# First-read touch, K of the first tile by chunks, a tile copied by two engines, and two more product slots, in an attention-plus-gated-MLP kernel

## The chip, the cores and the metric

The kernel runs on one core of one Trainium2 chip. The time is device microseconds of an execution. Spans inside a profile count from the first instruction of the profiled execution to the last, and are some 2 us shorter than the execution's time (269.8 us beside 271.54 for the profiled run of the kernel before).

PE is the matrix engine, DVE the vector engine, ACT the scalar engine, POOL the general one. SP issues most transfers. PSUM is the memory whose banks PE writes its results to, SBUF the working memory of all engines.

## The reference

```python
xn = layernorm(x)                      # x: [1, 2048, 640] bf16
q, k, v = split(xn @ wqkv)             # 32 heads of 20; wqkv: [640, 1920]
# each position s sees 8 keys: s, s-2, ..., s-14
attn = softmax(q . k[s - 2*w] * 20**-0.5)
A = (sum over w of attn * v[s - 2*w]) @ wo
B = ((xn @ w_gate) * (xn @ w_up)) @ w_down    # 640 -> 1536 -> 640
out = x + A + B
```

## The kernel before

The program has its own scheduler: while it is built, it estimates when each task could start, and so fixes the order of instructions on every engine. The program hands each engine its instructions in that order, with waits on semaphores between them. The order therefore matters as much as the work.

The start. Tiles of 128 rows of `x` and the columns of `wqkv` for Q, K and V are loaded on one queue, in this order. The small "touch" reads 64 bytes of every fifth row of `wqkv` in advance, on the queue of ACT, with no other use:

```python
    x_load(0)
    tch = A_wqkv.rearrange("(p r) n -> p r n", r=NCH)[:, 0, 0:32]
    stores.append(dma(TCH[:], tch, w=[TCH[:]], name="touch", eng="act"))
    x_load(1)
    wqkv_load(0, 0, 3)       # Q columns, chunks 0 to 2 of 5 (480 KB)
    wqkv_load(0, 3, NCH)     # Q columns, chunks 3 and 4 (320 KB)
    x_load(2)
    wqkv_load(1)             # K columns, all five chunks (800 KB)
    x_load(3)
```

A tile is normalised on DVE and ACT (`stats` in two halves, then `aggr`, `sqrt`, `recip`, `apply`), transposed by PE into PSUM and copied to SBUF (`XNT`) by DVE. Then PE makes Q and K from it.

The middle. For each block j of 512 positions, DVE multiplies Q with shifted views of K into "product slots" of 4 KB per partition, and PE sums them over the head by matmuls with a 0/1 matrix (`logits`, the line of `G`). For the last block, j = 3, DVE writes 16 half-size products in fp32 (`PRF`), which are summed pairwise: four sums by transfers with an adding destination, the others by POOL. Each product needs a free slot, and a slot comes free when a sum has read it:

```python
                for c in (c0, c0 + 1):
                    yield lambda: len(hold[c]) > 0 and len(usable(j)) > 0
                    k = slot(j)
                    ...
                    yield Task("dve", go, r=[q, rk], w=[o[:]], prio=20 + j)
    def sum32(j, r, q0, p, a, b):
        x, y = PRD32[a][:], PRD32[b][:]
        if (r, q0) in BY_DMA[p]:
            yield Task("pool", lambda: op("pool", lambda e: e.dma_start(x, y, accum_op=ALU.add), ...))
        else:
            yield calm
            yield Task("pool", lambda: op("pool", lambda e: e.tensor_tensor(x, x, y, ALU.add), ...))
        free.append(b)
```

At the same time PE computes the gate and up matmuls of the MLP (`WG`, `WU`), and DVE multiplies them (`HT`), which frees their PSUM banks.

Of the kernel before, what the change touches and what calls it, by code (L numbers as in the profile page):

```python
# [4 lines left out]
BF16 = mybir.dt.bfloat16  # L5
# [44 lines left out]
class Sched:  # L50
# [77 lines left out]
    def op(self, eng, fn, r=(), w=(), dma=False, name="", occ=None, lat=None, lock=False, nbytes=0, mode=0, group=None, extra=0.0, acc=0.0):  # L128
        X = _Op()
        X.eng, X.fn, X.name, X.dma, X.group = eng, fn, name, dma, group  # L130
        X.needs_tick, X.event, X.pre_know, X.idx = False, None, None, len(self.ops)
        X.nth = self.n_eng[eng]
        self.n_eng[eng] += 1
        rk = [k for a in r for k in self.keys(a)]
        wk = [k for a in w for k in self.keys(a)]
        deps = self.deps_of(eng, rk, wk)
        if occ is None and not dma:
            occ = 0.1
        inorder = eng in ("pe", "act", "dve")
        start = max([self.t[eng]] + [d.end for d in deps.values()])  # L140
        if lock:
            start = max(start, self.t_lock)
        if eng == "pe" and mode != self.pe_mode:
            start += 0.1
            self.pe_mode = mode
        if dma:
            self.t[eng] = start + (0.48 if occ is None else occ)
            if acc:
                self.t_acc = max(self.t_acc, start + 2.8) + acc
                X.end = self.t_acc  # L150
            else:
                self.t_data = max(self.t_data, start + 1.2) + nbytes / 280e3
                X.end = self.t_data + 0.8 + extra
        else:
            self.t[eng] = start + occ
            X.end = start + (occ if lat is None else lat)
        if lock:
            self.t_lock = start + occ
        last = {}
        keep = []  # L160
        for d in deps.values():
            if d.dma or d.eng == "pool":
                keep.append(d)
            else:
                b = last.get(d.eng)
                if b is None or b.idx < d.idx:
                    last[d.eng] = d
        X.deps = keep + list(last.values())
        for d in X.deps:
            if not d.dma:  # L170
                d.needs_tick = True
        for k in rk:
            st = self.state.get(k)
            if st is None:
                self.state[k] = [None, [X]]
            elif inorder and st[1] and st[1][-1].eng == eng and not st[1][-1].dma:
                st[1][-1] = X
            else:
                st[1].append(X)
        for k in wk:  # L180
            self.state[k] = [X, []]
        if dma:
            if group is None or group not in self.groups:
                sem = self.nc.alloc_semaphore(f"dma{self.n_dma}")
                self.n_dma += 1
                if group is not None:
                    self.groups[group] = [sem, []]
            if group is None:
                X.event = (sem, 16)
            else:  # L190
                g = self.groups[group]
                g[1].append(X)
                X.event = (g[0], 16)
        self.ops.append(X)
        return X
# [151 lines left out]
def build_kernel(nc, A_x, A_wqkv, A_wo, B_x, B_w_gate, B_w_up, B_w_down, out):  # L347
# [58 lines left out]
    ATX = [ATX0, sb("ATX1", [128, 2, 2, JB])]  # L406
    PRD += [sb("PRD10", [128, 4, JB], at=place[0] - 4096), sb("PRD11", [128, 4, JB], at=place[0])]
    NPR = len(PRD)
    PRD32 = [K.sbuf(f"PRF{i}", [128, 2, JB], FP32, K.base[p.name]) for i, p in enumerate(PRD)]
    QUAD = {3: (1, 0)}  # L410
    BY_DMA = (((0, 0), (0, 2)), ((1, 0), (1, 2)))
# [9 lines left out]
    MV = sb("MV", [128, NT, 2], FP32)  # L421
    SD = sb("SD", [128, NT, 4], FP32)
    DUM = sb("DUM", [128, 16], FP32)
    TCH = sb("TCH", [128, 32])
    ZERO = sb("ZERO", [128, JB])
    EPSC = sb("EPSC", [128, 16], FP32)
    IDENT = sb("IDENT", [128, 128])
# [15 lines left out]
    def mark(*k):  # L443
        done.add(k)
# [84 lines left out]
    def front(t):  # L529
# [5 lines left out]
        def stats(i):  # L535
            o, a = st[:, 6 * i:6 * i + 6], x[:, i * DHALF:(i + 1) * DHALF]
            op("dve", lambda e: e.bn_stats(o, a), r=[a], w=[("st", t, i)], name=f"bn{t}_{i}", occ=0.49)  # L537
# [25 lines left out]
        if t == 1:  # L563
            yield have("sd", 0)
        for i in range(2):
            yield Task("dve", lambda: stats(i), r=[x], prio=-1 if t == 1 and i == 0 else p)
        yield Task("dve", aggr, r=[("st", t, 1)], prio=p)
        yield Task("act", sqrt, r=[("mv", t)], prio=p - 1)
# [5 lines left out]
        if t < N_PE_T:  # L574
            hold = []

            def trans(b):
                tpv = PS[:, b, :].bitcast(BF16)[:, 0:NCH * 128].rearrange("p (c f) -> p c f", c=NCH)
                for c in range(NCH):
                    i, q = xs[:, c * 128:(c + 1) * 128], tpv[:, c, :]  # L580
                    op("pe", (lambda q, i: lambda e: e.transpose(q, i, IDENT[:]))(q, i), r=[i, IDENT[:]], w=[q],  # L581
                       name=f"tr{t}_{c}", occ=0.057, lat=0.2)
                hold.append((b, tpv))
                if t == 0:
                    warm(3)

            def copy():
                b, tpv = hold[0]
                if t < N_DVE_C:
                    X = op("dve", lambda e: e.tensor_copy(o, tpv), r=[tpv], w=[o], name=f"xntcp{t}", occ=0.49)  # L590
                else:
                    X = op("act", lambda e: e.activation(o, tpv, ACT.Copy), r=[tpv], w=[o], name=f"xntcp{t}", occ=0.75)
                K.free_bank(b, X)

            yield Task("pe", trans, r=[xs], prio=p, banks=1)
            yield Task("dve" if t < N_DVE_C else "act", copy, r=[PS[:, hold[0][0], :]], prio=p)
        else:
            def dmat():
                op("sp", lambda e: e.dma_start_transpose(o, xs), r=[xs], w=[o], dma=True, name=f"dtr{t}", nbytes=200e3, occ=1.25, extra=1.3)

            yield Task("sp", dmat, r=[xs], prio=1)
# [9 lines left out]
            return WQKV[:, WPOS[2], c, m * 128:(m + 1) * 128]  # L611
        return WQKV[:, WPOS[which], c, m:D:NCH]

    def mms(parts, b, name):
        order = [(p, c) for p in parts for c in range(NCH)]
        if name == "p0_0":
            order.sort(key=lambda t: t[1])
        for k, ((o, which, m, s0, n), c) in enumerate(order):
            if True:
                first = c == 0  # L620
                l, x = wcols(which, c, m), XNT[:, c, s0:s0 + n]
                op("pe", (lambda o, l, x, c, first: lambda e: e.matmul(o, l, x, start=first, stop=(c == NCH - 1)))(o, l, x, c, first),  # L622
                   r=[l, x], w=[o], name=f"{name}_{m}_{c}", occ=n / 2400 + 0.0024, lat=0.3)
# [16 lines left out]
    def proj_group(items, s0, n, prio, keys):  # L640
        hold = []

        def spread(*bs):
            b = bs[0]
            assert list(bs) == list(range(b, b + 4))
            mms([(PS[:, x, 0:n], 0, k, s0, n) for k, x in enumerate(bs)], b, "p0_0")
            hold.append((b, [(qk_dst(0, 0, 4, s0, n), PS[:, b:b + 4, 0:n], 4 * n)]))

        def go(b):
            parts, outs, col = [], [], 0  # L650
# [15 lines left out]
                    for u in range(n // TS):  # L666
                        bump("qk", which, (s0 + u * TS) // JB, m0 + k)

        w0 = wcols(items[0][0], NCH - 1, 0)
        wide = prio == FIRST  # L670
        yield Task("pe", spread if wide else go, r=[w0, XNT[:, NCH - 1, s0 + n - TS:s0 + n]], prio=prio, banks=4 if wide else 1, contig=wide)
        yield Task("act", ev, r=[o for _, o, _ in hold[0][1]], prio=5)

    def proj_qk():
        for pair in (0, 2):
            for which in (0, 1):
                for t in (pair, pair + 1):
                    yield have("xnt", t)
                    K.spawn(proj_group([(which, 0, 4)], t * TS, TS, FIRST if t + which == 0 else 10, None))
            for which in (0, 1):  # L680
                K.spawn(proj_group([(which, 4, 1)], pair * TS, 2 * TS, 10.2, None))
        for t in (4, 6):
# [152 lines left out]
    def sum32(j, r, q0, p, a, b):  # L835
        x, y = PRD32[a][:], PRD32[b][:]
        name = f"qsum{j}_{r}_{q0}_{p}"
        if (r, q0) in BY_DMA[p]:
            yield Task("pool", lambda: op("pool", lambda e: e.dma_start(x, y, accum_op=ALU.add), r=[x, y], w=[x], dma=True,
                                          name=name, occ=0.88, acc=3.3), r=[x, y], w=[x], prio=4)  # L840
        else:
            yield calm
            yield Task("pool", lambda: op("pool", lambda e: e.tensor_tensor(x, x, y, ALU.add), r=[x, y] + tokens(), w=[x],  # L843
# [24 lines left out]
    def logits(j, slots):  # L868
# [32 lines left out]
                        m = LOG[0][0:32, 0, 4 * r + s, 0:DIL * w]  # L901
                        op("pool", (lambda m: lambda e: e.memset(m, NEG))(m), w=[m], name=f"mask{w}", occ=0.2)  # L902

        yield Task("pe", go, r=[e[1][:] for e in slots], prio=9.5, banks=2, slack=0.5)
        bump("lg")
        for r in (1, 0):
            yield Task("act", lambda: ev(r), r=[PS[:, hold[1 - r], :]], w=[dst(r)], prio=2)
# [2 lines left out]
    def softmax(x):  # L910
# [47 lines left out]
        yield Task("dve", recip, r=[s3], prio=10)  # L958
        yield Task("dve", attn, r=[R], w=[L[:]], prio=10, lock=True)
        mark("sm", x)  # L960
        yield Task("sp", move, r=[L[:]], prio=4)

    NU = NJ * NCH
# [281 lines left out]
    N_PE_T = 5  # L1245
    N_DVE_A = 6
    N_DVE_C = 5
    FIRST = 9
    GU_KEEP = 3
    HP_MAX = 2  # L1250
# [5 lines left out]
    FIN_PRIO = 8  # L1256

    x_load(0)
    tch = A_wqkv.rearrange("(p r) n -> p r n", r=NCH)[:, 0, 0:32]
    stores.append(dma(TCH[:], tch, w=[TCH[:]], name="touch", eng="act"))  # L1260
    x_load(1)
    wqkv_load(0, 0, 3)
    wqkv_load(0, 3, NCH)
    x_load(2)
    wqkv_load(1)
    x_load(3)
    K.t["act"] = 2.1
    warm(18)
# [69 lines left out]
```

## Time and profile before

The kernel before took 271.62 us (median of 3 runs, 271.34 to 272.56).

| | before |
|---|---|
| PE, DVE, ACT, POOL busy | 97%, 83%, 39%, 48% |
| chain of waits, by engine | PE 86%, DMA 5%, POOL 3% |
| PE time lost in the first 10 us | 2.1 us in three gaps |
| PE time lost from 100 to 116 us | 1.6 us in three gaps |

First, two lines of the page: busy time with its share of the span and instruction count, for each engine; then the chain of work that ended last, by engine.

```profile
PE 262.3 (97%) x1765; PEld 152.2 (56%) x1783; DVE 223.3 (83%) x283; ACT 104.6 (39%) x186; POOL 129.2 (48%) x80
...
PE 86%; DMA 5%; POOL 3%; DVE 2%; issue 2%; ACT 0%; SPq 0%; POOLq 0%; ACTq 0%
```

PE is the limit nearly all the time. But a busy share says little here: the Trainium skill, "Trainium Kernel Development and Optimization", section "Performance Expectations", warns that matmul busy time is a bad metric for how close a kernel is to the roofline, because matmuls are pipelined. So I also took, from the trace, each matmul's start minus the start before it, less the usual spacing. The Trainium skill, "TensorE: Matmul & The Clock Gate", section "Wait — 56ns, not 53.3ns?", gives that spacing, once the array is at full clock, as N / 2.4 GHz plus about 2.5 ns, 55.6 and 215.7 ns for 128 and 512 columns. This trace agrees (granted clock 1.00): the commonest spacings are 56 and 216 ns. Whatever exceeds them is called "lost" below. An apparent gap of 0.22 us, at multiples of about 49 matmuls, is left out. It is a missing record, not idle time: 0.216 us is the spacing of one more matmul.

The list of PE's waits: what was waited for, us in total, times, the longest.

```profile
...
PE PS L1127 <- DVE HT L1136: 0.7, 2, 0.6
PE PS L622 <- DMA WQKV<-in_A_wqkv_dram: 0.7, 1, 0.7
PE PS L622 <- DVE XNT L590: 0.6, 1, 0.6
...
PE PS L883 <- POOL PRD L861: 0.3, 1, 0.3
```

The stretches 0 to 10 and 90 to 120 us of the same run: length, then busy us and instructions of PE, weight load, DVE, ACT and POOL, then PE's clock, the DMA share and GB/s.

```profile
0.00:10.00 10.00, 7.14 (x67) 5.41 (x68) 5.58 (x17) 2.75 (x5) 1.30 (x10) 1.00 0.79 253
...
90.00:120.00 30.00, 28.82 (x143) 12.57 (x144) 20.62 (x25) 9.62 (x17) 16.53 (x9) 1.00 0.64 143
```

PE lacks 2.86 of 10 us at the start and 1.18 of 30 us in the second stretch. (1.27 us of the former is the start before the first instruction.)

The start in the timeline, DVE first: start, duration, instruction, count, and in brackets the idle time before it with what ended it.

```profile
...
7.97 0.49 DVE L537 BATCH_NORM_STATS2 STATS<-XST 128x6 f32<-128x320 bf16 x1 [0.52 <-DMA XST<-in_A_x_dram]
8.55 0.49 DVE L590 COPY XNT<-PS 128x640 bf16<-128x640 bf16 x1
```

And PE in the same stretch:

```profile
...
6.86 1.37 PE L622 MATMUL PS<-XNT,WQKV 128*128 128x128 bf16 x20 [0.73 <-DMA WQKV<-in_A_wqkv_dram]
8.07 0.44 PE L581 MATMUL PS<-IDENT,XNS 128*128 128x128 bf16 x5
9.10 1.09 PE L622 MATMUL PS<-XNT,WQKV 128*128 128x128 bf16 x16 [0.59 <-DVE XNT L590]
```

The first Q matmul waits for its weights (6.86). The Q matmuls of tile 1 (9.10) wait for the copy of tile 1, which DVE does at 8.55. Before that copy in DVE's order is the first half of tile 2's statistics, which waits 0.52 us for the load of tile 2 and ends at 8.47. In PE's order it is the transposes of tile 1, which the copy reads: they come after the 20 Q matmuls of tile 0 and end at 8.51. So PE's transposes ended last, and the chain of waits goes through them (start, us, what):

```profile
...
6.86 1.37 PE PS L622 x20
8.23 0.29 PE PS L581 x5
8.52 0.02 issue
8.55 0.50 DVE XNT L590
```

The middle of the kernel, DVE, then PE:

```profile
...
100.56 1.23 DVE L817 TENSOR_TENSOR PRF<-PS,KT 128x1024 f32<-128x1024 f32 x1 [3.05 <-DMA PRF<-PRF]
101.70 0.68 DVE L1136 TENSOR_TENSOR HT<-HT,PS 128x512 bf16<-128x512 bf16 x1
103.08 1.22 DVE L817 TENSOR_TENSOR PRF<-PS,KT 128x1024 f32<-128x1024 f32 x1 [0.70 <-DMA PRF<-PRF]
...
106.33 1.23 DVE L817 TENSOR_TENSOR PRF<-PS,KT 128x1024 f32<-128x1024 f32 x1 [0.84 <-DMA PRF<-PRF]
```

```profile
...
102.66 1.03 PE L1127 MATMUL PS<-XNT,WU 128*128 128x512 bf16 x4 [0.55 <-DVE HT L1136]
...
115.94 0.40 PE L883 MATMUL PS<-PRD,G 128*32 128x512 bf16 x4 [0.34 <-POOL PRD L861]
```

DVE stands still for 3.05, 0.70 and 0.84 us, because the next product has no free slot before an adding transfer has landed. The products `HT` that stand behind it in DVE's order come late, PE's PSUM banks stay taken, and PE waits 0.55 us at 102.66 (0.72 lost). At 115.94 the last logits group waits for POOL (0.34 idle, 0.50 lost).

### The profile page before, as it was taken

How to read it: one execution, taken by the hardware profiler on the slowest of the kernel's cores; microseconds unless marked ns; L12 is line 12 of the kernel's file. 1: busy time of each engine (PE TensorE's matmuls, PEld its weight loads, DVE VectorE, ACT ScalarE, POOL GpSimd, SP SyncE). 2: the span in 40 equal slices, each digit the busy share in tenths (PEclk: the TensorE clock that was granted, in tenths of full speed). 3: DMA queues.
4: the chain of work that ended last, by engine and by line, in shares of the span. 5: the costliest groups of instructions: out<-in, count | busy, mean ns of one | idle time of the engine just before them, and what ended most of it. 6: DMA issues, size and time to landing. Idle time of an engine off the chain costs nothing.

```text
span 269.8 us, 4454 instructions
## 1 busy us (share of the span) xinstructions
PE 262.3 (97%) x1765; PEld 152.2 (56%) x1783; DVE 223.3 (83%) x283; ACT 104.6 (39%) x186; POOL 129.2 (48%) x80
## 2 busy tenths in 40 slices
PE   6899999999999998999999999999999999999996
PEld 4896965544444443434444446764467644776775
DVE  4788899999999957489998989999999899982212
ACT  2369998557632122345334362025320342202000
POOL 1000000000006418910499999888999789974000
PEclk9999999999999999999999999999999999999999
DMA  6955479422325996059027933575426750031301
GB/s 198 367 200 93 97 96 390 179 97 90 112 43 142 231 238 147 0 181 235 12 53 169 228 88 93 157 183 137 107 77 176 190 148 2 0 97 51 95 29 49
DMA packets 40293, 35.58 MB, mean 132 GB/s; under 512 B 15440, under 2 KB 38480, under 8 KB 40272
## 3 DMA queue, kind: packets, MB, share of 16 engines
q1 hardware_dynamic: 39408, 33.15, 45.2%
q0 software_dynamic: 576, 2.10, 3.9%
q8 instruction: 14, 0.23, 0.4%
q10 hardware_dynamic: 288, 0.05, 0.1%
q14 instruction: 7, 0.06, 0.1%
HBM read 25.08 MB, written 5.26 MB: 112 GB/s over the span
## 4 chain that ended last, share of the span: by engine, by line
PE 86%; DMA 5%; POOL 3%; DVE 2%; issue 2%; ACT 0%; SPq 0%; POOLq 0%; ACTq 0%
PE PS L1127 29%; PE PS L1209 28%; PE PS L622 24%; DMA PRF<-PRF 3%; PE PS L883 3%; POOL PRD L861 2%; PE PS L1076 2%; DMA WQKV<-in_A_wqkv_dram 2%; DVE PRF L817 1%; POOL PRF L843 1%; DVE HT L1136 1%; PE PS L581 0%; SPq L462 0%; ACT KT L627 0%; DVE XNT L590 0%
## 5 line engine op out<-in xcount | busy, mean ns | idle before, releaser
L1034 POOL TENSOR_TENSOR SV<-PV 128x1024 bf16<-128x1024 f32 x40 | 93.4, 2359 | 24.4 <-DVE LOG L936 16.0
L1029 DVE TENSOR_TENSOR PV<-VX,PS 128x1024 f32<-128x1024 bf16 (+1 forms) x56 | 92.1, 1671 | 0.4 <-ACT PS L1014 0.2
L622 PE MATMUL PS<-XNT,WQKV 128*128 128x512 bf16 (+2 forms) x475 | 66.4, 298 | 1.9 <-DMA WQKV<-in_A_wqkv_dram 0.7
L1127 PE MATMUL PS<-XNT,WU 128*128 128x512 bf16 x233 | 58.1, 379 | 1.0 <-DVE HT L1136 0.7
L1127 PE MATMUL PS<-XNT,WG 128*128 128x512 bf16 x234 | 58.7, 379 | 0.4
L622 PEld LDWEIGHTS PS<-XNT,WQKV 128*128 128x128 bf16 x480 | 43.4, 114 | 23.9 <-DVE XNT L590 1.1
L1127 PEld LDWEIGHTS PS<-XNT,WU 128*128 128x128 bf16 x240 | 23.2, 98 | 29.7 <-DVE HT L1136 1.5
L1127 PEld LDWEIGHTS PS<-XNT,WG 128*128 128x128 bf16 x240 | 23.3, 98 | 28.2 <-issue 0.4
L772 DVE TENSOR_TENSOR PRD<-QT,KT 128x2048 bf16<-128x2048 bf16 x32 | 36.7, 1220 | 0.0
L1222 DVE TENSOR_TENSOR FOUT<-PS,XR 128x320 bf16<-128x320 f32 (+1 forms) x33 | 15.8, 478 | 22.4 <-PE PS L1209 22.4
L1085 ACT ACTIVATE OT<-PS 128x512 bf16<-128x512 f32 x20 | 10.5, 599 | 48.5 <-PE PS L1076 48.5
L1209 PE MATMUL PS<-WD,HT 128*128 128x320 bf16 x192 | 28.7, 299 | 0.1
L627 ACT ACTIVATE HT<-PS 128x512 bf16<-128x512 f32 x24 | 14.3, 596 | 34.9 <-PE PS L1127 34.8
L1209 PE MATMUL PS<-WO,OT 128*128 128x320 bf16 (+1 forms) x165 | 27.1, 295 | 0.0
L843 POOL TENSOR_TENSOR PRF<-PRF,PRF 128x1024 f32<-128x1024 f32 x4 | 9.4, 2347 | 36.6 <-DVE PRF L817 36.6
L1209 PEld LDWEIGHTS PS<-WD,HT 128*128 128x128 bf16 x192 | 18.6, 98 | 8.2 <-issue 0.4
L817 DVE TENSOR_TENSOR PRF<-PS,KT 128x1024 f32<-128x1024 f32 x16 | 19.1, 1218 | 4.6 <-DMA PRF<-PRF 4.6
L902 POOL MEMSET LOG<- 32x6 bf16 (+6 forms) x7 | 0.4, 95 | 46.9 <-ACT LOG L894 46.9
L1136 DVE TENSOR_TENSOR HT<-HT,PS 128x512 bf16<-128x512 bf16 x23 | 15.5, 680 | 5.3 <-PE PS L1127 3.5
L1209 PEld LDWEIGHTS PS<-WO,OT 128*128 128x128 bf16 x165 | 15.8, 98 | 6.6 <-issue 0.8
L537 DVE BATCH_NORM_STATS2 STATS<-XST 128x6 f32<-128x320 bf16 x32 | 14.7, 469 | 2.4 <-DMA XST<-in_A_x_dram 2.4
L1209 PE MATMUL PS<-WD,XNT 128*128 128x320 bf16 (+1 forms) x108 | 14.5, 284 | 0.0
(57 smaller groups left out, 214.4 us busy)
## 6 DMA issues: line engine op xcount, KB each, us to landing
VX<-v_scratch SPq DMA_DIRECT2D x80, 130.0 KB, 3.0
XST<-in_A_x_dram SPq DMA_DIRECT2D x16, 160.0 KB, 6.5
v_scratch<-VST SPq DMA_DIRECT2D x4, 640.0 KB, 4.3
XR<-in_A_x_dram SPq DMA_DIRECT2D x16, 160.0 KB, 2.9
out_dram<-FOUT SPq DMA_DIRECT2D x15, 160.0 KB, 1.8
PRF<-PRF POOLq DMA_DIRECT2D x4, 512.0 KB, 9.4
WG<-in_B_w_gate_dram SPq DMA_DIRECT2D x1, 1920.0 KB, 7.7
WU<-in_B_w_up_dram SPq DMA_DIRECT2D x1, 1920.0 KB, 11.8
```

The source lines that it names most:

```text
L537: op("dve", lambda e: e.bn_stats(o, a), r=[a], w=[("st", t, i)], name=f"bn{t}_{i}", occ=0.49)
L622: op("pe", (lambda o, l, x, c, first: lambda e: e.matmul(o, l, x, start=first, stop=(c == NCH - 1)))(o, l, x, c, first), r=[l, x], w=[o], ...
L627: X = op("act", (lambda o, i: lambda e: e.activation(o, i, ACT.Copy))(o, i), r=[i], w=[o], name=name, occ=0.12 + n * 0.9e-3)
L772: op("dve", lambda e: e.tensor_tensor(s[:], qb, kv, ALU.mult), r=[q, rk], w=[s[:]], name=f"prod{j}_{r}_{c}", occ=1.15, lock=True)
L817: X = op("dve", lambda e: e.tensor_tensor(o[:], qb, kv, ALU.mult), r=[q, rk], w=[o[:]], name=f"prow{j}_{r}_{c}_{q0}", occ=1.17)
L843: yield Task("pool", lambda: op("pool", lambda e: e.tensor_tensor(x, x, y, ALU.add), r=[x, y] + tokens(), w=[x], name=name, occ=2.36, lock ...
L1029: op("dve", lambda e: e.tensor_tensor(p, vw, a, ALU.mult), r=[vv] + rk, w=[p], name=f"pv{u}_{x}_{r0}", occ=0.09 + 1.1 * nr)
L1034: X = op("pool", lambda e: e.tensor_tensor(o, p[:, :, 0, :], p[:, :, 1, :], ALU.add), r=[p[:]] + tokens(), w=[o], name=f"pva{u}_{x}", occ= ...
L1127: op("pe", (lambda l, x, c: lambda e: e.matmul(PS[:, b, :], l, x, start=(c == 0), stop=(c == NCH - 1)))(l, x, c), r=[l, x], w=[PS[:, b, :] ...
L1136: X = op("dve", lambda e: e.tensor_tensor(h, h, PS[:, hold[1], :], ALU.mult), r=[h, PS[:, hold[1], :]], w=[h], name=f"h{m}_{j}", occ=0.65)
L1209: op("pe", (lambda l, x, i: lambda e: e.matmul(dst, l, x, start=(i == 0), stop=(i == n - 1)))(l, x, i), r=[l, x], w=[PS[:, b, :]], name=f" ...
L1222: X = op("dve", lambda e: e.tensor_tensor(o, PS[:, b, 0:wid], xr, ALU.add), r=[PS[:, b, :], xr], w=[o], name=f"fin{t}_{nb}", occ=0.15 + wi ...
```

## The change

Its intent: (a) let each DMA engine touch a row of each chunk that it will later load; (b) K of tile 0 by chunks, as Q already is, to fill PE's waiting; (c) copy tile 0 with DVE (three chunks) and ACT (two) at once; (d) hold the second half of tile 2's statistics back behind the copy of tile 1; (e) two more product slots in memory of softmax 0 once that is done, a later assumed start (2.0 instead of 0.5 us) for the last logits group, and two constants of the scheduler's estimate of adding transfers. The core of the diff:

```diff
-                self.t_acc = max(self.t_acc, start + 2.8) + acc
+                self.t_acc = max(self.t_acc, start + 3.8) + acc
...
     NPR = len(PRD)
+    PRD += [sb("PRD12", [128, 4, JB], at=a_sc), sb("PRD13", [128, 4, JB], at=a_sc + 4096)]
...
         for i in range(2):
+            if t == 2 and i == 1:
+                yield have("xnt", 1)
             yield Task("dve", lambda: stats(i), r=[x], prio=-1 if t == 1 and i == 0 else p)
...
-            yield Task("pe", trans, r=[xs], prio=p, banks=1)
-            yield Task("dve" if t < N_DVE_C else "act", copy, r=[PS[:, hold[0][0], :]], prio=p)
+            yield Task("pe", trans, r=[xs], prio=p, banks=2 if t < N_SPLIT else 1)
+            if t < N_SPLIT:
+                yield Task("act", lambda: part(3, NCH, "act"), r=[PS[:, hold[1][0], :]], prio=p - 1)
+                yield Task("dve", lambda: part(0, 3, "dve"), r=[PS[:, hold[0][0], :]], prio=p - 1)
...
-        wide = prio == FIRST
+        wide = prio < 10
...
+        if wide:
+            yield Task("pe", spread, r=[wcols(items[0][0], NCH - 1, 0)], prio=prio)
...
-                                          name=name, occ=0.88, acc=3.3), r=[x, y], w=[x], prio=4)
+                                          name=name, occ=0.88, acc=3.4), r=[x, y], w=[x], prio=4)
...
-        yield Task("pe", go, r=[e[1][:] for e in slots], prio=9.5, banks=2, slack=0.5)
+        yield Task("pe", go, r=[e[1][:] for e in slots], prio=9.5, banks=2, slack=2.0 if j in QUAD else 0.5)
...
         mark("sm", x)
+        if x == 0:
+            free.extend((12, 13))
...
-    tch = A_wqkv.rearrange("(p r) n -> p r n", r=NCH)[:, 0, 0:32]
-    stores.append(dma(TCH[:], tch, w=[TCH[:]], name="touch", eng="act"))
+    tch = A_wqkv.rearrange("(c k p) n -> k c p n", k=16, c=NCH)[:, :, 0, 0:32]
+    stores.append(dma(TCH[0:16], tch, w=[TCH[0:16]], name="touch", eng="act"))
...
-    wqkv_load(1)
+    wqkv_load(1, 0, 3)
+    wqkv_load(1, 3, NCH)
```

More of the change, by code (lines that the diff above doesn't have):

```diff
@@ L423, in build_kernel @@
     DUM = sb("DUM", [128, 16], FP32)
-    TCH = sb("TCH", [128, 32])
+    TCH = sb("TCH", [128, NCH, 32])
     ZERO = sb("ZERO", [128, JB])
@@ L575, in front, with trans, part @@
             hold = []
-            def trans(b):
-                tpv = PS[:, b, :].bitcast(BF16)[:, 0:NCH * 128].rearrange("p (c f) -> p c f", c=NCH)
+            def trans(*bs):
+                tpvs = [PS[:, b, :].bitcast(BF16)[:, 0:NCH * 128].rearrange("p (c f) -> p c f", c=NCH) for b in bs]
+                b, tpv = bs[0], tpvs[0]
                 for c in range(NCH):
-                    i, q = xs[:, c * 128:(c + 1) * 128], tpv[:, c, :]
+                    i, q = xs[:, c * 128:(c + 1) * 128], tpvs[c // 3 if len(bs) > 1 else 0][:, c, :]
                     op("pe", (lambda q, i: lambda e: e.transpose(q, i, IDENT[:]))(q, i), r=[i, IDENT[:]], w=[q],
                        name=f"tr{t}_{c}", occ=0.057, lat=0.2)
-                hold.append((b, tpv))
+                hold.extend(zip(bs, tpvs))
                 if t == 0:
                     warm(3)
+            def part(lo, hi, eng):
+                b, tpv = hold[lo // 3]
+                a, i = o[:, lo:hi], tpv[:, lo:hi]
+                if eng == "dve":
+                    X = op("dve", lambda e: e.tensor_copy(a, i), r=[PS[:, b, :]], w=[a], name=f"xntcp{t}_0", occ=0.1 + 0.08 * (hi - lo))
+                else:
+                    X = op("act", lambda e: e.activation(a, i, ACT.Copy), r=[PS[:, b, :]], w=[a], name=f"xntcp{t}_1",
+                           occ=0.12 + 0.12 * (hi - lo))
+                K.free_bank(b, X)
             def copy():
@@ L593, in copy @@
                 K.free_bank(b, X)
-            yield Task("pe", trans, r=[xs], prio=p, banks=1)
-            yield Task("dve" if t < N_DVE_C else "act", copy, r=[PS[:, hold[0][0], :]], prio=p)
+            yield Task("pe", trans, r=[xs], prio=p, banks=2 if t < N_SPLIT else 1)
+            if t < N_SPLIT:
+                yield Task("act", lambda: part(3, NCH, "act"), r=[PS[:, hold[1][0], :]], prio=p - 1)
+                yield Task("dve", lambda: part(0, 3, "dve"), r=[PS[:, hold[0][0], :]], prio=p - 1)
+            else:
+                yield Task("dve" if t < N_DVE_C else "act", copy, r=[PS[:, hold[0][0], :]], prio=p)
         else:
@@ L612, in wcols, with mms @@
         return WQKV[:, WPOS[which], c, m:D:NCH]
-    def mms(parts, b, name):
+    def mms(parts, b, name, outer=None):
         order = [(p, c) for p in parts for c in range(NCH)]
-        if name == "p0_0":
-            order.sort(key=lambda t: t[1])
+        if outer is not None:
+            order = [(p, c) for c in outer for p in parts]
         for k, ((o, which, m, s0, n), c) in enumerate(order):
@@ L643, in spread @@
         def spread(*bs):
-            b = bs[0]
-            assert list(bs) == list(range(b, b + 4))
-            mms([(PS[:, x, 0:n], 0, k, s0, n) for k, x in enumerate(bs)], b, "p0_0")
-            hold.append((b, [(qk_dst(0, 0, 4, s0, n), PS[:, b:b + 4, 0:n], 4 * n)]))
+            if bs:
+                hold.append((bs[0], [(qk_dst(items[0][0], 0, 4, s0, n), PS[:, bs[0]:bs[0] + 4, 0:n], 4 * n)]))
+            b, which = hold[0][0], items[0][0]
+            mms([(PS[:, b + k, 0:n], which, k, s0, n) for k in range(4)], b, f"p{which}_0", range(0, 3) if bs else range(3, NCH))
         def go(b):
@@ L667, in ev @@
                         bump("qk", which, (s0 + u * TS) // JB, m0 + k)
-        w0 = wcols(items[0][0], NCH - 1, 0)
-        wide = prio == FIRST
+        wide = prio < 10
+        w0 = wcols(items[0][0], 2 if wide else NCH - 1, 0)
         yield Task("pe", spread if wide else go, r=[w0, XNT[:, NCH - 1, s0 + n - TS:s0 + n]], prio=prio, banks=4 if wide else 1, contig=wide)
+        if wide:
+            yield Task("pe", spread, r=[wcols(items[0][0], NCH - 1, 0)], prio=prio)
         yield Task("act", ev, r=[o for _, o, _ in hold[0][1]], prio=5)
@@ L678, in proj_qk @@
                     yield have("xnt", t)
-                    K.spawn(proj_group([(which, 0, 4)], t * TS, TS, FIRST if t + which == 0 else 10, None))
+                    K.spawn(proj_group([(which, 0, 4)], t * TS, TS, FIRST + 0.5 * which if t == 0 else 10, None))
             for which in (0, 1):
@@ L1247, in build_kernel @@
     N_DVE_C = 5
+    N_SPLIT = 1
     FIRST = 9
```

## The prediction

> **What bounds the kernel.** TensorE. The page gives PE 97% busy, DVE 83%, ACT 39%, POOL 48%, and the chain of waits is 86% PE. So the change can only win the time in which PE stands still. By matmul starts minus the steady spacing of their shape, PE loses about 2.1 us in the first 10 us (0.44 at the first transposes, 0.89 before the first Q matmul at 6.86, 0.75 before the Q matmuls of tile 1 at 9.10) and about 1.6 us between 102 and 116 us (0.72 and 0.35 waiting for the DVE product of HT, 0.50 in the last logits group waiting for POOL's PRD sum). Elsewhere nothing exceeds 0.34. So 3.7 us are to be won; 2% would need 5.4.
>
> **The touch and the chunked K load.** The first Q matmul waits for WQKV. In the landing records of that 480 KB load, the median of 16 engines is in at 5.47 and the last at 6.72; later loads inherit this straggler (tile 2 of x: 6.74 and 7.95). Packet records show why: 1280-byte packets take 55 ns, but between 3.0 and 5.1 us some twenty take 200 to 850. The old touch reads every fifth row[...]. The Trainium skill, "DMA: Bandwidth & Descriptors", section on why a DMA increments its semaphore by 16, says that the slowest dimensions decide over how many engines a copy is spread; so 16 partitions by 5 chunks should give each engine a row of each of its own chunks. No run here shows that yet. If first reads are the cause, the load lands near 5.6 to 6.0. I count this half likely.
>
> **Tile 0 copied by two engines.** The DVE copy is 0.49 us (timeline, 5.84 to 6.33). Three of five chunks should take about 0.34 and begin after the third transpose; ACT's two about 0.37 beside it. The first Q matmul, if its weights are there, begins near 6.15, not 6.86. But K of tile 0 follows Q of tile 1 in the new order, so much of this goes to waiting for tile 1. Its copy follows statistics of tile 2, which waited 0.52 us for the straggling load; without the straggler Q of tile 1 begins near 8.5 instead of 9.1, otherwise near 8.95. ACT is 98 to 100% busy from 25 to 35 us and may take some of it back. Expected 0.5 us, at most 1.
>
> **Two more product slots.** DVE waits 4.6 us, three times (3.05, 0.70, 0.84), for the summing DMAs (7.2 to 10.1 us each) to free a slot, between 97 and 107 us; HT products queue behind and stop PE. In the new order products 14 to 16 wait for sums 1 to 3, instead of 13 to 15 for 2 to 4: waits nearly vanish. POOL's sums should end near 112.5, not 115.9. PE wins about 1.1 of its 1.6.
>
> **Prediction.** 0.5 + 1.1 us: 270.0 us, range 269.0 to 271.3. Faster by over 2%: 0.01; within 2%: 0.98; slower: 0.01.
>
> **What would show it.** Landings of the first WQKV load: last near median, long packets gone; first Q matmul before 6.5. DVE wait on PRF DMAs under 1 us; no PE wait on HT; PE busy share 98%; PE idle under 6 us in all.
>
> **What would make it wrong.** The touch stalling x itself; long packets having another cause; the PE time won early being lost to ACT evictions before 40 us; the new schedule placing some instruction before its data, with a new PE wait after 120 us.

## The result, and the profile after

The changed kernel took 270.30 us (median of 6 runs, 270.01 to 270.63), the kernel before 271.68 us in the same rounds (6 runs, 271.03 to 272.56). Ratios here are the mean time of one kernel's fast runs over that of the other's in the same rounds, so not quite the ratio of the medians. Here it is 0.9949, with a 95% interval of 0.9930 to 0.9967: faster by 0.5%, which is clear of noise and well within 2%.

The same two lines of the page, for the changed kernel (line numbers are some 20 higher in this file):

```profile
PE 262.7 (98%) x1765; PEld 152.8 (57%) x1783; DVE 222.9 (83%) x282; ACT 105.4 (39%) x188; POOL 130.3 (48%) x81
...
PE 94%; DMA 2%; DVE 2%; issue 1%; SPq 0%; DVEq 0%
```

Its list of PE's waits, with the stretch of the `HT` wait and POOL's gone:

```profile
...
PE PS L640 <- DVE XNT L604: 0.6, 1, 0.6
PE PS L640 <- DMA WQKV<-in_A_wqkv_dram: 0.5, 1, 0.5
...
```

The same two stretches:

```profile
0.00:10.00 10.00, 7.47 (x57) 5.21 (x58) 5.23 (x16) 2.77 (x5) 1.30 (x10) 1.00 0.80 259
...
90.00:120.00 30.00, 29.84 (x149) 13.36 (x150) 21.61 (x26) 9.83 (x17) 17.27 (x10) 1.00 0.73 174
```

The second stretch is full now: 29.84 of 30 us, against 28.82. The first lacks 2.53 us, no clear gain. The start in the timeline, DVE, then PE:

```profile
...
5.96 0.36 DVE L595 COPY XNT<-PS 128x384 bf16<-128x384 bf16 x1 [0.20 <-PE PS L585]
...
8.49 0.49 DVE L538 BATCH_NORM_STATS2 STATS<-XST 128x6 f32<-128x320 bf16 x1 [1.05 <-DMA XST<-in_A_x_dram]
9.09 0.49 DVE L604 COPY XNT<-PS 128x640 bf16<-128x640 bf16 x1
```

```profile
...
7.30 1.48 PE L640 MATMUL PS<-XNT,WQKV 128*128 128x128 bf16 x20 [0.53 <-DMA WQKV<-in_A_wqkv_dram]
8.61 0.44 PE L585 MATMUL PS<-IDENT,XNS 128*128 128x128 bf16 x5
9.64 0.53 PE L640 MATMUL PS<-XNT,WQKV 128*128 128x128 bf16 x6 [0.59 <-DVE XNT L604]
```

The tile-0 copy is shorter (0.36 us on DVE), yet the first Q matmul starts at 7.30, later than before, and Q of tile 1 at 9.64. The load of tile 2 lets DVE wait 1.05 us before 8.49, but again PE's transposes, which begin at 8.61, end last (9.06, the statistics 8.98).

The middle, DVE, then PE:

```profile
...
102.46 1.22 DVE L837 TENSOR_TENSOR PRF<-PS,KT 128x1024 f32<-128x1024 f32 x1
...
104.79 1.23 DVE L837 TENSOR_TENSOR PRF<-PS,KT 128x1024 f32<-128x1024 f32 x1 [0.37 <-DMA PRF<-PRF]
```

```profile
...
116.51 1.05 PE L903 MATMUL PS<-PRD,G 128*32 128x512 bf16 x16
```

DVE waits only once, 0.37 us, PE never, and the 16 logits matmuls of the last group run in one piece at 116.51.

So the profile says at once that the gain came from the slots and the start gave nothing. But one profile is one draw, and the start looks like a draw of luck. The experiments take the two apart.

### The profile page after: what moved, and what is told of

It is laid out like the page before. It is cut to its first block, busy times and chain, and to the rows that moved or that the text cites. A ratio compares the mean times of both kernels' runs of the same rounds, so it can differ in the third digit from the quotient of the medians.

```text
span 268.9 us, 4464 instructions
## 1 busy us (share of the span) xinstructions
PE 262.7 (98%) x1765; PEld 152.8 (57%) x1783; DVE 222.9 (83%) x282; ACT 105.4 (39%) x188; POOL 130.3 (48%) x81
## 4 chain that ended last, share of the span: by engine, by line
PE 94%; DMA 2%; DVE 2%; issue 1%; SPq 0%; DVEq 0%
PE PS L1149 36%; PE PS L1231 28%; PE PS L640 24%; PE PS L903 3%; DMA WQKV<-in_A_wqkv_dram 2%; PE PS L1098 2%; DVE HT L1158 1%; PE PS L585 0%; DVE RS L952 0%; DVE LOG L956 0%; SPq L463 0%; DVE XNT L604 0%; DVE SM L932 0%; DVE FOUT L1244 0%; DVEq L325 0%
## 5 line engine op out<-in xcount | busy, mean ns | idle before, releaser
L1149 PE MATMUL PS<-XNT,WU 128*128 128x512 bf16 x239 | 59.6, 380 | 0.2
L1149 PE MATMUL PS<-XNT,WG 128*128 128x512 bf16 x229 | 57.3, 380 | 0.7 <-issue 0.3
L1158 DVE TENSOR_TENSOR HT<-HT,PS 128x512 bf16<-128x512 bf16 x24 | 16.3, 680 | 8.7 <-PE PS L1149 7.0
```

Source lines behind the costliest of these rows:

```text
L1149: op("pe", (lambda l, x, c: lambda e: e.matmul(PS[:, b, :], l, x, start=(c == 0), stop=(c == NCH - 1)))(l, x, c), r=[l, x], w=[PS[:, b, :] ...
L1158: X = op("dve", lambda e: e.tensor_tensor(h, h, PS[:, hold[1], :], ALU.mult), r=[h, PS[:, hold[1], :]], w=[h], name=f"h{m}_{j}", occ=0.65)
```

## The experiments

All runs of 5 rounds have 6 timed runs of the kernel and 11 of the kernel before, which is shared among the kernels that ran together (e1 to e4; e5 to e8; e9 and e10).

**A measure that holds in all of them.** In each trace I read three times: the last landing of tile 2's load ("x2", semaphore records), the first Q matmul of tile 1 ("Q1"), and the end of the last matmul.

| kernel | first Q weights | x2 | Q1 | Q1 − x2 | end − Q1 |
|---|---|---|---|---|---|
| before | 6.72 | 7.95 | 9.10 | 1.15 | 258.37 |
| changed | 7.17 | 8.46 | 9.64 | 1.18 | 256.88 |
| e5, changed again | 7.04 | 8.37 | 9.54 | 1.17 | 256.87 |
| e1, late part only | 6.19 | 7.43 | 8.70 | 1.27 | 256.98 |
| e2, early part only | 6.02 | 7.28 | 8.62 | 1.34 | 258.42 |
| e3, changed, old touch | 7.40 | 8.69 | 9.85 | 1.16 | 256.87 |
| e4, changed, no touch | 6.28 | 7.51 | 8.80 | 1.29 | 256.87 |
| e6, slots alone | 7.04 | 8.35 | 9.45 | 1.10 | 257.38 |
| e7, x2 earlier | 6.36 | 6.79 | 8.26 | 1.47 | 256.87 |
| e8, statistics held back | 7.04 | 8.32 | 8.88 | 0.56 | 256.87 |
| e9, e7 with the touch | 7.02 | 7.45 | 8.87 | 1.42 | 256.87 |
| e10, e7 again | 6.18 | 6.60 | 8.19 | 1.59 | 256.88 |

The last column falls into three classes and hardly varies inside one: 258.4 without the late part, 257.4 with the slots alone (one trace), 256.9 to 257.0 with the whole late part. After Q1 the late part alone decides. Before Q1, up to e6, Q1 comes 1.1 to 1.3 us after x2, in the old order and in the new one, and x2 wanders by more than a microsecond from run to run.

That is no proof that Q1 follows x2, as I took it when I planned e7 and e8. In the same rows x2 itself comes 1.2 to 1.3 us after the first Q weights, so Q1 keeps a distance from these too (2.4 to 2.6 us). The traces decide: in all eight, the copy of tile 1 begins 0.04 us after PE's transposes of tile 1 end, while DVE's statistics of tile 2 had ended 0.03 to 0.27 us before the copy: before the transposes in seven traces, and together with them in e6. And the time that PE loses just before Q1 is 0.75 us in all eight, wherever x2 falls. Where DVE was free early, the profile names PE's transposes as what the copy waited for, as in e4:

```profile
...
7.53 0.49 DVE L538 BATCH_NORM_STATS2 STATS<-XST 128x6 f32<-128x320 bf16 x1 [0.27 <-DMA XST<-in_A_x_dram]
8.26 0.49 DVE L604 COPY XNT<-PS 128x640 bf16<-128x640 bf16 x1 [0.23 <-PE PS L585]
```

So up to e6 Q1 follows the Q weights: PE waits for them, does the 20 Q matmuls of tile 0, then the transposes of tile 1, and then has nothing to do until the copy is made.

**e1, late part only, and e2, early part only.** The edit of e1 is the four late pieces of the diff put into the kernel before; e2 is the changed kernel with the same pieces taken out:

```diff
+    PRD += [sb("PRD12", [128, 4, JB], at=a_sc), sb("PRD13", [128, 4, JB], at=a_sc + 4096)]
+        if x == 0:
+            free.extend((12, 13))
-        yield Task("pe", go, ..., slack=0.5)
+        yield Task("pe", go, ..., slack=2.0 if j in QUAD else 0.5)
```

> The kernel before with only the late part of the change: two more product slots, the later start of the last logits group, and the scheduler's two constants. Theory (the whole gain comes from the product slots, the early part gives nothing): about 270.2 us, 1.4 under before, with no PE loss above 0.3 between 90 and 120 us and DVE waits on the summing DMAs under 1 us. Rival (the gain is shared, half from the start of the kernel): about 271.0 us.

> The changed kernel without the slots, the later logits start and the two constants; so the new touch, K of tile 0 by chunks, tile 0 copied by two engines. Theory: within 0.3 us of before, 271.4 to 271.9, with the PE losses near 100 to 116 us still there. Rival (shared gain): about 270.9.

Measured: e1 269.93 us (ratio to before 0.9953, 0.9936 to 0.9971), e2 271.63 us (1.0020, 0.9999 to 1.0041); before 271.29 in the same rounds. e1 has the whole gain, e2 none. In e2 the loss in the middle is still there, as one wait:

```profile
...
102.90 1.25 PE L1146 MATMUL PS<-XNT,WU 128*128 128x512 bf16 x5 [1.38 <-DVE HT L1155]
```

This first rival, a shared gain, is refuted.

**e3, old touch, and e4, no touch.** Only the touch differs from the changed kernel; the order on every engine is otherwise the same.

```diff
-    tch = A_wqkv.rearrange("(c k p) n -> k c p n", k=16, c=NCH)[:, :, 0, 0:32]
-    stores.append(dma(TCH[0:16], tch, w=[TCH[0:16]], name="touch", eng="act"))
+    tch = A_wqkv.rearrange("(p r) n -> p r n", r=NCH)[:, 0, 0:32]                 # e3 only
+    stores.append(dma(TCH[:, 0], tch, w=[TCH[:, 0]], name="touch", eng="act"))    # e3 only
```

> The changed kernel with the old touch (128 partitions, every fifth row); the order on every engine is the same but for that one load. If the new touch is worth something, this is slower than the changed kernel by 0.3 to 0.7 us (270.6 to 271.0) and its first weight load has more packets over 150 ns between 3 and 5 us. If the touch's shape doesn't matter: 270.3 within 0.2.

> The changed kernel without any touch. If a first read by an engine is what costs, and a touch takes it over: slower than the changed kernel by 0.5 us or more, with clearly more time lost in long packets of the first weight load than the 7.3 us of the changed kernel (sum over packets between 3 and 5 us). If the long packets have another cause: the same time within 0.2, the same sum, and one engine still 1 to 2 us late.

Measured: e3 270.04 us (0.9959, 0.9940 to 0.9979), e4 269.75 us (0.9943, 0.9926 to 0.9961). Neither is slower than the changed kernel. e4 looks 0.3 to 0.5 us faster, but the intervals overlap; e9 and e10 decide. The new shape shows no worth against the old, and no touch is no worse. The packets of 1,280 bytes between 3 and 5 us say the same: 17 over 150 ns and 7.3 us above the usual time in the changed kernel, 25 and 10.6 in its second trace (e5), 22 and 10.2 in e3, 22 and 6.4 in e4.

**e5, the changed kernel again, and e6, the slots alone.** e6 is the kernel before with only the two lines of slots and the line that frees them; the logits start and the constants are the old ones.

> The changed kernel unaltered, as a control on the same chip as the next three. Expected 270.3 within 0.3. If the start of the kernel is set by the last landing of the tile-2 load of x, its first Q matmul of tile 1 begins 1.1 to 1.4 us after that landing in this trace too, and PE's chain ends about 256.9 us after that matmul.

> The kernel before with nothing but the two more product slots: no later start of the last logits group, old constants. If the slots alone do it, 269.9 to 270.3 and no PE loss above 0.3 us from 90 to 113; if the later start of the logits is needed too, a loss of 0.3 to 0.6 us stays at that group near 113 us, and the time is 270.4 to 270.8.

Measured: e5 270.34 us (0.9964, 0.9930 to 0.9998), e6 270.68 us (0.9973, 0.9943 to 1.0003). e5's range, 269.63 to 271.95, is wider than expected. In its slowest run and in the slowest of the kernel before in these rounds (273.64) the granted clock was 0.994; without these two the ratios of e5 to e8 would be 0.9961, 0.9981, 0.9934 and 0.9940. e6's gain in time is not clear of noise; what the slots are worth rests on its trace. e6 keeps a loss at the last logits group, where PE, 12 of 16 matmuls in, waits for POOL's last sum:

```profile
...
114.27 0.83 PE L884 MATMUL PS<-PRD,G 128*32 128x512 bf16 x12
115.31 0.40 PE L884 MATMUL PS<-PRD,G 128*32 128x512 bf16 x4 [0.21 <-POOL PRD L862]
```

That is 0.37 us lost. By the last column of the table the slots give 258.37 − 257.38 = 0.99 us, and the later logits start with the constants another 257.38 − 256.87 = 0.51 us. The latter two were not run apart.

**e7, tile 2 loaded earlier, and e8, statistics held back.** The theory when they were planned: DVE's fixed order hands the delay of tile 2's load on to the copy of tile 1, hence to PE. Both kernels have no touch, and have tile 1 transposed before the second part of Q of tile 0, so they undo PE's order and DVE's at once. e7 then loads tile 2 earlier, e8 puts both halves of its statistics behind the copy.

```diff
+                mark("tr", t)                      # at the end of trans
...
         if wide:
+            if items[0][0] == 0:
+                yield have("tr", 1)
             yield Task("pe", spread, r=[wcols(items[0][0], NCH - 1, 0)], prio=prio)
...
     wqkv_load(0, 0, 3)
+    x_load(2)                                      # e7 only
     wqkv_load(0, 3, NCH)
-    x_load(2)                                      # e7 only
...
-            if t == 2 and i == 1:
+            if t == 2 and i == 0:                  # e8 only
```

> The changed kernel without touch, with the x load of tile 2 issued before the second part of the Q weights, and tile 1 transposed before the second part of Q of tile 0. If the order of DVE (statistics of tile 2 before the copy of tile 1) hands the late load's delay on to PE, Q of tile 1 begins near 8.4 us instead of 8.6 to 9.9, and the time is 269.2 to 269.6. Rival (PE's start does not matter because a later stage absorbs it): 269.8 or more, though Q begins earlier.

> The changed kernel without touch, with both halves of tile 2's statistics after the copy of tile 1, and tile 1 transposed before the second part of Q of tile 0. By the same theory Q of tile 1 begins near 8.4 whatever tile 2's load does; tile 2 is then normalised later, and PE may lose up to 0.4 us at its transposes near 10.7. Expected 269.3 to 269.8; the spread of its runs smaller than that of the changed kernel (0.6 us).

Measured: e7 269.34 us (0.9927, 0.9897 to 0.9956; runs 269.23 to 269.63), e8 269.51 us (0.9931, 0.9904 to 0.9959; runs 269.29 to 269.84). e7's start, PE, then DVE:

```profile
...
6.50 0.84 PE L641 MATMUL PS<-XNT,WQKV 128*128 128x128 bf16 x12 [0.42 <-DMA WQKV<-in_A_wqkv_dram]
7.22 0.45 PE L585 MATMUL PS<-IDENT,XNS 128*128 128x128 bf16 x5
7.73 2.46 PE L641 MATMUL PS<-XNT,WQKV 128*128 128x128 bf16 x39
```

```profile
...
7.07 0.49 DVE L538 BATCH_NORM_STATS2 STATS<-XST 128x6 f32<-128x320 bf16 x1
7.71 0.49 DVE L605 COPY XNT<-PS 128x640 bf16<-128x640 bf16 x1
```

DVE no longer waits for tile 2. PE has the 8 matmuls of the second part of Q of tile 0 to do while DVE copies tile 1, and from 7.22 goes on with at most small gaps. Q1 comes at 8.26. The rival, that a later stage absorbs PE's start, is refuted: end − Q1 is 256.87 as in the changed kernel. In e8 DVE stood free and the copy of tile 1 waited for PE's transposes:

```profile
...
8.34 0.49 DVE L605 COPY XNT<-PS 128x640 bf16<-128x640 bf16 x1 [1.16 <-PE PS L585]
```

PE lost nothing at tile 2's transposes, so the feared 0.4 us did not come. But Q1 came at 8.88, not near 8.4: as before Q1 follows the Q weights, now by 1.84 to 2.01 us (e7 to e10) instead of 2.37 to 2.60, and they came at 7.04 in e8. The gain of some 0.5 us is about the 8 matmuls (0.45 us at 56 ns) that now run beside the copy.

Neither edit was run alone. An estimate from the traces: holding the statistics back in the old order would have won next to nothing, as the copy already began 0.04 us after PE's transposes there. Transposing tile 1 early alone would have left the copy waiting for the statistics; in e8, where tile 2 landed at 8.32, half of them takes 0.49 us, so to some 8.8 instead of 8.34. So both seem to be needed together.

**e9, touch put back into e7, and e10, e7 again.**

> The kernel of e7 (tile 2 of x loaded earlier, tile 1 transposed earlier, no touch) with the new touch put back; the order on every engine is otherwise the same. If the touch is worth nothing and only takes time from the first loads: 0.1 to 0.4 us slower than the same kernel without it (next run). If it helps once the order lets it: 0.2 us faster or more.

> The kernel of e7 again, as the control of the run before on the same chip: 269.2 to 269.6 expected, the fastest of all, with a range of its runs under 0.6 us.

Measured, side by side: e9 269.56 us, e10 269.56 us, both 0.9944 to before. In this order the touch is worth nothing and costs nothing that six runs show. The landings of the first Q weights say the same: 6.18 to 7.04 in the four traces without a touch (e4, e7, e8, e10), 6.02 to 7.40 in the eight with one. So I take e4's apparent gain for the luck of its draws, not for the missing touch; that is not shown, as the old order was not repeated without it. e10 was 0.2 us slower than e7, inside its expected range of medians; its runs spread 0.71 us, more than the 0.6 I had expected.

**e11 and e12, the same loads twice.** These test the premise of the touch: that the long packets at the start are first reads. The changed kernel without touch does its first seven loads, waits until all have landed, and does them again. In e11 the first pass reads the same addresses, in e12 rows of the same length from two other weights. The result is right in both; the extra 12 us (281.47 and 282.05 beside e4's 269.75) are on purpose. Abridged:

```diff
+    for each of the first seven loads: dma(same destination, same source)   # e11; e12: w_down, w_up as sources
+    dma(TCH[0:16, 0], A_wo[0:16, 0:32], r=first, w=[TCH[0:16, 0]], name="pre_done")
     x_load(0)
```

> The changed kernel without touch, with its first seven loads done once beforehand, into the same places, and again only when all have landed (some 9 us longer on purpose). If it is the first read of an address that makes packets long, the second pass of the same seven loads has under 1.5 us in all above the usual 55 ns, where the first pass has 8 to 15, and its last engine lands within 0.3 us of the median. If any burst of these loads has long packets, both passes look alike.

> As e11, but the first pass reads rows of the same length from other tensors, so the second pass still reads its own rows for the first time, on engines that have already worked. If first reads of an address cost: the second pass has 8 to 15 us above 55 ns, as much as the first pass. If it is only the engines' or the memory's start: under 1.5 us, as in e11.

From the packet records, 1,664 packets of 1,280 bytes in a pass, in order of start, median 55 ns in all passes; "above" is the sum of what exceeds 55 ns:

```
                       packets over 150 ns   above, us   longest, ns
e11 first pass                 44               16.7          948
e11 second pass, same data     56               16.9          871
e12 first pass, other data     38               15.6         1182
e12 second pass                46               16.1         1331
before, old touch              41               15.2         1393
changed, new touch             42               14.6         2049
e4, no touch                   55               16.5          779
```

Reading the same bytes a second time is no better than the first. So the long packets are not first reads, and no touch can remove them. What they are stays open. The Trainium skill, "DMA: Bandwidth & Descriptors", section "Latency and other measured facts", gives an HBM access latency of 0.2 us on average and 2 us at high load; the long packets are of that size (0.15 to 2.05 us), and the DMA engines are busy in these microseconds (DMA share 0.97 to 1.06 from 4 to 10 us in the kernel before), but no run here shows that this is the cause.

## Why the prediction was right or wrong

The time was right, 270.0 predicted and 270.30 measured, but by the luck of two errors that nearly cancelled: the early 0.5 us was not there, and the late 1.1 us was 1.5.

- *"So the change can only win the time in which PE stands still."* Right. Every difference after Q1 is a loss that went away.
- *"If first reads are the cause, the load lands near 5.6 to 6.0. I count this half likely."* Wrong, and this is the step that failed. The first Q weights landed at 7.17 and 7.04 in the two traces of the changed kernel, later than the 6.72 before, with one packet of 2,049 ns. e11 shows that the cause is not a first read; in e9 and e10 the medians with and without the touch are the same. I had seen long packets at the first load and taken "first" for the reason. That the touch's rows fall on the engines that load them later was my inference. The Trainium skill, "DMA: Bandwidth & Descriptors", section "Why a DMA increments its semaphore by 16 and not by 1", on which the prediction leans, says how the slowest dimensions decide over the number of engines that a copy uses; which rows each of them gets does not follow from that. Packet records here name no engine, so whether the new touch did what (a) intends stays open; with e11 it does not matter.
- *"The first Q matmul, if its weights are there, begins near 6.15."* They were not there. In e2 and e4, with weights at 6.02 and 6.28, it began at 6.41.
- *"without the straggler Q of tile 1 begins near 8.5 instead of 9.1, otherwise near 8.95."* Wrong in its path. I had let the copy of tile 1 follow the statistics of tile 2. It followed PE's transposes of tile 1, which stand behind all 20 Q matmuls of tile 0 and so behind both parts of the Q weights, whatever is won on the copy of tile 0; the statistics had ended 0.03 to 0.27 us before the copy began. PE lost 0.75 us there before the change and after it. With the straggler Q of tile 1 began at 9.64, not 8.95; with early weights at 8.62 (e2) and 8.80 (e4), in the old order too at 8.70 (e1). Expected 0.5 us; by e1 and e2, nothing. (The chunked K and the copy by two engines were not run alone.)
- *"ACT … may take some of it back."* Refuted: end − Q1 is 256.9 wherever Q1 falls between 8.19 and 9.85.
- *"waits nearly vanish"*. Right. DVE's wait for adding transfers went from 4.6 us in three waits to 0.4 us in one, as the list of DVE's waits between 90 and 120 us shows, before and after:

```profile
...
DVE PRF L817 <- DMA PRF<-PRF: 4.6, 3, 3.0
```

```profile
...
DVE PRF L837 <- DMA PRF<-PRF: 0.4, 1, 0.4
```

- *"PE wins about 1.1 of its 1.6."* The mechanism was right, the size too small: the late part gave 1.49 us (258.37 − 256.88), 0.99 of it by the slots. I had left out a term for the later logits start, which with its constants gave 0.5 us: the last group then starts when POOL is done (sums to 114.38, group from 116.51).
- *"POOL's sums should end near 112.5."* They ended at 114.38, but on a clock that ran later: in the changed kernel DVE's first product began at 35.25, not 33.85. With the late part alone (e1, first product at 33.45) they ended at 112.41.
- *"PE busy share 98%"* and *"no PE wait on HT"*: right. *"PE idle under 6 us in all"*: narrowly missed in this trace, 268.9 − 262.7 = 6.2 us, from which 18 matmul records are missing; in e5's trace of the same kernel, with all 1,783, it is 268.8 − 264.0 = 4.8 us. *"first Q matmul before 6.5"*: missed, 7.30.

A version better than both came out of it: the changed kernel with the touch dropped, tile 2 loaded before the second part of Q's weights, and tile 1 transposed before the second part of Q of tile 0 (e7 and e10). Its 12 runs took 269.17 to 269.88 us, those of the changed kernel 269.63 to 271.95. The second and third edit were not run apart, and in time it is not clear of e4, the changed kernel with the touch dropped and nothing else (269.39 to 269.98, in other rounds): that the order itself gains some 0.5 us is read from the traces, by Q1 and the Q weights.

## What to carry to other kernels

Before you remove a wait near the start, follow the queues of all engines that hand over next, and ask which ends last. Here the copy of tile 1 waited on DVE behind half a tile of statistics and on PE behind 20 matmuls; the idle time in DVE's row drew the eye, but PE's transposes ended last, by 0.04 to 0.23 us (in e6 the two ended together). Two milestones that keep a fixed distance (x2 and Q1) need not be cause and effect, when both follow a third. A delay that varies from run to run is no effect until several traces show it; a milestone after it (here, from Q1 to the end) can be exact to 0.1 us where the total varies by 1. And test a premise such as "first reads are slow" by doing the same thing twice.

## What the Trainium skill lacked or had wrong

- "DMA: Bandwidth & Descriptors" has no figure for how unevenly packets are served while several loads from SP are queued: with a median of 55 ns for 1,280 bytes, 38 to 56 of 1,664 packets took over 150 ns in the seven passes above and single ones up to 2,049 ns, so the last of the 16 completions of one 480 KB load came 0.6 to 1.9 us after their median (e2: 6.02 and 5.46; e3: 7.40 and 5.47). Later loads on the queue kept the lag (tile 2 of x in the kernel before: median 6.74, last 7.95).
- No page says whether touching memory ahead helps. Here it did not: second reads had 16.9 us above the usual packet time, first reads 16.7, and the time with and without a touch was 269.56 us in both.
- "DMA: Bandwidth & Descriptors", section "Anatomy of one DMA — SWDGE (gpsimd) path", fits 2.0 us plus bytes / 436 GB/s for a DMA; from it I estimate some 3.2 us for 512 KB. The adding transfers of 512 KB on that path took 7.2 to 10.1 us from issue to landing in the kernel before, up to three of them in flight. The page has no figure for adding transfers.
